# K as the moving operand, row softmax and two score banks in a decode kernel that streams a key/value cache

## The chip, the cores and the metric

The kernel runs on one core of one Trainium2 chip. The metric is the device time of one execution in microseconds. A core has five engines that matter here: TensorE (PE, with its weight loads as PEld), VectorE (DVE), ScalarE (ACT), GpSimd (POOL) and SyncE (SP), which issues every DMA of this kernel. SBUF and PSUM are the two on-chip memories, each of 128 partitions[...].

## The reference

Two transformer layers with the same weights and the same cache, for one new token of each of 8 batches:

```python
def _A_ref(x, k_cache, v_cache, wq, wo):
    q = (x @ wq).reshape(B, 1, 32, 128).transpose(0, 2, 1, 3)
    scores = jnp.einsum("bhqd,bhkd->bhqk", q, k_cache) * (128 ** -0.5)
    p = softmax(scores, axis=-1)
    o = jnp.einsum("bhqk,bhkd->bhqd", p, v_cache)
    return o.transpose(0, 2, 1, 3).reshape(B, 1, 32 * 128) @ wo
def _B_ref(x, w1, w2):
    return jnp.maximum(x @ w1, 0) @ w2
x = x + _A_ref(_layernorm(x), K, V, wq, wo)
x = x + _B_ref(_layernorm(x), w1, w2)
x = x + _A_ref(_layernorm(x), K, V, wq, wo)
x = x + _B_ref(_layernorm(x), w1, w2)
```

B is 8, the model width D is 640, there are 32 heads of width 128 with 4096 keys each, and the feed-forward width is 1728. Everything is bf16. K and V together are 537 MB, and each of the two layers needs all of them.

## The kernel before

The work is cut into visits. A visit (layer, batch, pair of heads) takes the K tile and the V tile of two heads; there are 2 x 8 x 16 = 256 visits. Each tile is cut into four granules of 512 KB, 2048 bf16 values in each of the 128 partitions. The arena in SBUF has room for G = 26 granules, and the whole cache goes through it, a load (L546) taking one to eight granules that lie side by side.

A planner, `plan` (L34), writes out the order of all operations by hand, and every engine gets its part in that order. It walks over the visits: K of visit i, then V of visit i-1. After each granule that is not kept it releases the place and, where it can, issues the next load (`release`, `feed`). Between granules, `step` puts in pieces of the small work from a list of chains. After K of a visit its chain is T, M2, B, E, L, I; after V it is OG, O and, by layer, W and Y, and at the end of a layer the feed-forward part (`finish`, L186). `until` forces the pieces that must be out before the next step.

The planner keeps 21 granules of a batch from layer 0 in the arena for layer 1 (`keep`), and 3 more (STASH) outside it: each is copied out into six half-granule tiles, five PSUM banks and one SBUF tile called annex (`do_stash`, L534), and copied back just before its use (`do_unstash`, L543). So layer 1 of a batch reads 24 granules less. The visits of a batch's layer 1 begin with the head pairs that were kept; between the end of layer 0 and there stand the first two visits of the next batch (AHEAD = 2), beside which the feed-forward part of layer 0 runs.

The scores: `do_mm` (L572) takes 128 keys of K at a time as the weight (128x128) and the head's q as a moving operand of one column, 16 matmuls for a granule (L590), into one column each of the score tile `s_ps`, 128 keys down the partitions and 64 columns, 32 for each head. `s_ps` holds two visits by turns in one tile. For V (L578), P is the weight, four columns at a time, and V moves with 512 columns: four matmuls for a granule on four column tiles of the array (`tile_position`), into `o_ps`.

The softmax: M1 (L596, DVE) takes the maximum over the columns; T (L599, PE) turns it into two rows; M2 (L603, L605, DVE) takes their maximum and puts it on a 2x2 diagonal; B (L608, PE) spreads it to all partitions; E scales it (L614, ACT) and takes the exponential, once per head (L618), which gives `P_sb` in the layout that V's matmuls need. L (L623, PE) sums the columns over the partitions, I (L629, L633, DVE) adds up and inverts. OC (L637, ACT) copies `o_ps` out, OG (L642, PE) gathers its diagonal pieces, O (L652, DVE) multiplies by the inverse sum, W (L659, PE) projects with `wo`, Y (L676, DVE) adds to x. In layer 1, Q (L564) makes the two heads' q and QC (L570, ACT) copies it to `qo`.

Of the kernel before, what the change touches and what calls it, by code (L numbers as in the profile page):

```python
# [20 lines left out]
STASH = 3  # L21
# [12 lines left out]
def plan(B, NP, n_up, n_down):  # L34
# [26 lines left out]
    stash = first[G - SPARE : G - SPARE + STASH]  # L61

# [25 lines left out]
    ops, chains = [], []  # L88
# [6 lines left out]
    def stashed(which, i, g):  # L95

        x = which, visits[i][2], g
        return stash.index(x) if x in stash else None

# [9 lines left out]
    def feed():  # L109

        while at[0] < len(stream):
# [4 lines left out]
            while n < most and place(stream[at[0] + n]) == (b, p + n, keeping):  # L116
                n += 1
# [12 lines left out]
            ops.append(("load", b, p, n, u))  # L130
# [5 lines left out]
    def release(which, i, g):  # L136
# [7 lines left out]
        if visits[i][0] == 0 and stashed(which, i, g) is not None:  # L144
            ops.append(("stash", stashed(which, i, g), u))
        owner[u], freed[u] = False, at[1]
# [34 lines left out]

    def query(b, n):

        return [(10, ("Q", b, order1[n])), (0, ("QC", b, order1[n]))]
# [18 lines left out]
    for which, i in slots:  # L203
        layer, b, hp = visits[i]
        if which == "K":
            if layer == 0 and b == 0 and hp % GP == 0:
                ops.append(("Q0", hp // GP))
            if layer:
                until(("QC", b, hp))
                if order1.index(hp) + 2 < NP:  # L210
                    chains.append(query(b, order1.index(hp) + 2))
        else:
            until(("E", i))
            clock[0] = max(clock[0], ready.pop(i))
# [7 lines left out]
        if which == "K":  # L222
# [5 lines left out]
            chains.append([(1, ("T", i)), (0, ("M2", i)), (1, ("B", i)), (0, ("E", i)), (1, None), (1, ("L", i)), (0, ("I", i))])  # L228
# [27 lines left out]
def kernel(  # L256
# [26 lines left out]
    GJ = GW // P  # L283
# [64 lines left out]
    ones_b = _free(onesb_c[:2], [(0, P)])  # L348
# [11 lines left out]
    qo = consts.tile([P, B, H], BF16, name="qo")  # L360
    wo_sum = sm.tile([P, 2, 2, 2], BF16, name="wo_sum", bufs=1)
    OR = 96 + CJ
    o_ps = ps.tile([P, CJ * Dh], FP32, name="o_ps")
    s_ps = ps.tile([P, 2, 2 * NJ], FP32, name="s_ps")
    small_ps = ps.tile([P, BANK], FP32, name="small_ps")
    oy_ps, sum_ps, mean_ps, var_ps = (small_ps[:, lo:hi] for lo, hi in ((0, 48), (48, 56), (64, 72), (72, 80)))
    turn_ps, max_ps, q1_ps = small_ps[:2, 80 : 80 + P], small_ps[:, 208:210], small_ps[:, 212:216]
    lsum_ps, ffn_ps, row_ps = small_ps[:, 216 : 216 + 2 * NJ], small_ps[:, 280:440], small_ps[:, 280 : 280 + P]
    per = GW // (2 * BANK)
    stash = [ps.tile([P, 2 * BANK], BF16, name=f"stash{n}_ps") for n in range(STASH * per - 1)]  # L370
# [5 lines left out]
    s_tiles, P_tiles, m_tiles, o_tiles, oy, invL, oT, nmax, st = ({} for _ in range(9))  # L376
# [168 lines left out]
    def do_load(b, p, n, u):  # L545
        nc.sync.dma_start(out=arena[:, u * GW : (u + n) * GW], in_=A_kv[b, :, p * GW : (p + n) * GW])  # L546
# [22 lines left out]
    def take_q(b, hp):  # L569
        nc.scalar.copy(out=qo[:, b, 2 * hp : 2 * hp + 2], in_=st.pop(("q", b, hp)))  # L570

    def do_mm(which, i, g, u):  # L572
# [11 lines left out]
        if g == 0:  # L584
            s_tiles[i] = s_ps[:, i % 2]
        h = 2 * hp + g * 2 // UNIT
        q = qo[:, b, h : h + 1]
        for n in range(GJ):
            j = g * GJ + n
            nc.tensor.matmul(  # L590
                s_tiles[i][:, j : j + 1], lhsT=arena[:, at + n * P : at + (n + 1) * P], rhs=q, start=True, stop=True
            )

    def do_m1(i):
        m_tiles[i] = sm.tile([P, 2], BF16, name="mrow")
        nc.vector.tensor_reduce(out=m_tiles[i], in_=s_tiles[i].rearrange("p (h j) -> p h j", h=2), axis=AX.X, op=ALU.max)  # L596

    def do_t(i):
        nc.tensor.matmul(turn_ps, lhsT=m_tiles.pop(i), rhs=ident, start=True, stop=True)  # L599

    def do_m2(i):
        hmx = sm.tile([2, 1], FP32, name="hmx")
        nc.vector.tensor_reduce(out=hmx, in_=turn_ps, axis=AX.X, op=ALU.max)  # L603
        nmax[i] = sm.tile([2, 2], BF16, name="diag")
        nc.vector.tensor_tensor(out=nmax[i], in0=ident[:2, :2], in1=_free(hmx, [(0, 2)]), op=ALU.mult)  # L605

    def do_b(i):
        nc.tensor.matmul(max_ps, lhsT=ones_b, rhs=nmax.pop(i), start=True, stop=True)  # L608

    def do_e(i):  # L610
        nm = sm.tile([P, 2], FP32, name="nmax")
        layer, b, hp = visits[i]
        less, more = (q_scale[b][:, 1:2], q_scale[b][:, 0:1]) if layer else (-inv_sqrt_dh, inv_sqrt_dh)
        nc.scalar.activation(out=nm, in_=max_ps, func=ACT.Copy, scale=less)  # L614
        P_tiles[i] = sm.tile([P, 2, NJ], BF16, name="P_sb")
        S = s_tiles.pop(i).rearrange("p (h j) -> p h j", h=2)
        for h in range(2):
            nc.scalar.activation(  # L618
                out=P_tiles[i][:, h, :], in_=S[:, h, :], func=ACT.Exp, bias=nm[:, h : h + 1], scale=more
            )  # L620

    def do_l(i):
        nc.tensor.matmul(  # L623
            lsum_ps, lhsT=ones_p, rhs=P_tiles[i].rearrange("p h j -> p (h j)"), start=True, stop=True
        )

    def do_i(i):
        L = sm.tile([P, 2], FP32, name="lsum")
        nc.vector.tensor_reduce(  # L629
            out=L, in_=lsum_ps.rearrange("p (h j) -> p h j", h=2), axis=AX.X, op=ALU.add  # L630
        )
# [3 lines left out]
    def do_oc(i):  # L635
        o_tiles[i] = sm.tile([P, CJ, Dh], BF16, name="o_sb", bufs=1)
# [35 lines left out]
    def do_y(i):  # L672
# [6 lines left out]
                L=do_l, I=do_i, OC=do_oc, OG=do_og, O=do_o, W=do_w, Y=do_y, C=do_finish, Q0=do_q0, Q=do_q, QC=take_q)  # L679
# [17 lines left out]
def _laid_out(A_x, A_k_cache, A_v_cache, A_wq, A_wo, B_w1, B_w2):  # L697
# [9 lines left out]
    k = A_k_cache.reshape(B, NP, 2, Sk, Dh).transpose(0, 1, 4, 2, 3).reshape(B, NP, Dh, 2 * Sk)  # L707
# [39 lines left out]
```

## Time and profile before

| what | value |
| --- | --- |
| median of three runs | 2364.6 us (2361.87 to 2365.31) |
| profiled execution | 2369.0 us, of which 2367.1 us are the profile's span |
| TensorE matmuls busy | 1300.1 us, 55%; 26,522 instructions |
| TensorE weight loads busy | 796.9 us, 34%; 26,522 instructions |
| DVE, ACT, POOL busy | 393.9, 394.6 and 39.3 us |
| read from HBM | 988.08 MB, 417 GB/s over the span |
| loads into the arena | 536: 236 of 512 KB, 127 of 4096 KB, the rest between |

Times are microseconds from the start of the span. A group of the profile gives the line, the engine, the operation, what it writes and reads, how often, its busy time, the mean of one in nanoseconds, and the idle time of the engine ahead of it with the cause of its end. TensorE's matmuls overlap, and their ends are modelled: sixteen matmuls of 165 ns can lie within 0.56 us. A turn is the stretch, once per batch, in which layer 0 of the batch ends and its layer 1 begins; they lie near 205, 490, 785, 1070, 1365, 1645, 1945 and 2215 us.

### The profile page before, as it was taken

Reading aid. Unit: us, or ns where it says so; the run is one execution under the profiler, and the core shown is the slowest. Engines: PE = TensorE matmul, PEld = TensorE weight load, DVE = VectorE, ACT = ScalarE, POOL = GpSimd, SP = SyncE. Lnnn points to the kernel's source line nnn. Section 1 sums busy time; section 2 is a strip of 40 time slices with the busy share of each in tenths; the row PEclk is TensorE's granted clock in tenths of the full one; section 3 lists DMA queues with packets and bytes.
Section 4 is the critical chain, followed back from the end, with each engine's and each line's share of the span. In section 5 each row is a group of like instructions: output and inputs, shape, how many; then the busy total and the mean of one; then the engine's idle time right before and its main releaser. Section 6 shows DMA issues by size and latency. Waiting matters only on the chain.

```text
span 2367.1 us, 57911 instructions
## 1 busy us (share of the span) xinstructions
PE 1300.1 (55%) x26522; PEld 796.9 (34%) x26522; DVE 393.9 (17%) x1913; ACT 394.6 (17%) x1185; POOL 39.3 (2%) x190
## 2 busy tenths in 40 slices
PE   3437644575545854448444585446744466544855
PEld 2324322343323532225222353223422244222533
DVE  1112111121112211122111221112211122112211
ACT  1111211121111211112111121111211112111211
POOL 0000000000000000000000000000000000000000
DMA  9999999999999999999999999999999999999997
GB/s 409 428 430 385 433 428 433 429 387 433 429 432 428 392 433 429 433 425 391 432 431 431 416 406 432 430 430 408 423 432 431 430 404 427 432 431 428 383 432 303
DMA packets 78969, 991.83 MB, mean 419 GB/s; under 512 B 8836, under 2 KB 8836, under 8 KB 39044
## 3 DMA queue, kind: packets, MB, share of 16 engines
q1 hardware_dynamic: 78724, 988.13, 98.8%
q8 instruction: 207, 3.39, 0.5%
q14 instruction: 38, 0.31, 0.0%
HBM read 988.08 MB, written 0.01 MB: 417 GB/s over the span
## 4 chain that ended last, share of the span: by engine, by line
DMA 75%; PE 18%; ACT 3%; DVE 2%; issue 1%; SPq 0%; DVEq 0%; ACTq 0%
DMA arena<-in_A_kv_dram 75%; PE s_ps L590 8%; PE o_ps L578 4%; ACT P_sb L618 2%; PE small_ps L564 1%; PE small_ps L642 1%; ACT nmax L614 1%; PE small_ps L468 1%; DVE hmx L603 1%; PE small_ps L659 1%; PE small_ps L623 1%; PE small_ps L608 1%; PE small_ps L599 0%; PE small_ps L494 0%; DVE diag L605 0%
## 5 line engine op out<-in xcount | busy, mean ns | idle before, releaser
L578 PE MATMUL o_ps<-arena,P_sb 128*4 128x512 bf16 x4096 | 564.2, 600 | 595.9 <-DMA arena<-in_A_kv_dram 595.0
L590 PE MATMUL s_ps<-qo,arena 128*128 128x1 bf16 x16384 | 535.4, 165 | 381.6 <-DMA arena<-in_A_kv_dram 360.2
L590 PEld LDWEIGHTS <-arena 128*128 128x128 bf16 x16384 | 495.8, 104 | 406.2 <-DMA arena<-in_A_kv_dram 380.4
L578 PEld LDWEIGHTS <-P_sb 128*4 128x4 bf16 x4096 | 89.6, 81 | 665.1 <-issue 650.0
L614 ACT ACTIVATE nmax<-small_ps 128x2 f32<-128x2 f32 x128 | 22.0, 172 | 1047.2 <-PE small_ps L608 1047.2
L629 DVE TENSOR_REDUCE lsum<-small_ps 128x2 f32<-128x64 f32 x256 | 57.3, 224 | 715.4 <-PE small_ps L623 715.4
L637 ACT CAST o_sb<-o_ps 100x512 bf16<-100x512 f32 x256 | 149.8, 585 | 105.5 <-PE o_ps L578 102.6
L614 ACT ACTIVATE nmax<-small_ps,q_scale 128x2 f32<-128x2 f32 x128 | 33.5, 262 | 640.6 <-PE small_ps L608 640.6
L603 DVE TENSOR_REDUCE hmx<-small_ps 2x1 f32<-2x128 f32 x256 | 71.4, 279 | 312.2 <-PE small_ps L599 312.2
L596 DVE TENSOR_REDUCE mrow<-s_ps 128x2 bf16<-128x64 f32 x256 | 57.6, 225 | 380.1 <-PE s_ps L590 351.7
L623 PEld LDWEIGHTS <-onesb_c 128*128 128x128 bf16 x256 | 26.4, 103 | 199.3 <-issue 199.2
L618 ACT ACTIVATE P_sb<-s_ps,nmax,q_scale 128x32 bf16<-128x32 f32 x256 | 82.6, 373 | 4.2
L652 DVE TENSOR_TENSOR oT<-small_ps,invL 128x2 bf16<-128x2 f32 x128 | 20.3, 159 | 312.2 <-PE small_ps L642 312.2
L642 PE MATMUL small_ps<-gsel,o_sb 100*128 100x2 bf16 x1024 | 66.3, 169 | 8.3 <-DVE xc L511 1.8
L599 PE MATMUL small_ps<-ident,mrow 128*2 128x128 bf16 x256 | 70.5, 276 | 0.2 <-DVE mrow L596 0.2
L564 PE MATMUL small_ps<-xq,wq_sb 128*128 128x1 bf16 x1280 | 52.1, 165 | 32.1 <-DVE qo L652 26.8
L564 PEld LDWEIGHTS <-wq_sb 128*128 128x128 bf16 x1280 | 52.9, 104 | 45.3 <-issue 44.4
L608 PEld LDWEIGHTS <-onesb_c 2*128 2x128 bf16 x256 | 25.2, 98 | 116.0 <-issue 115.7
L623 PE MATMUL small_ps<-P_sb,onesb_c 128*128 128x64 bf16 x256 | 57.2, 223 | 8.8
L618 ACT ACTIVATE P_sb<-s_ps,nmax 128x32 bf16<-128x32 f32 x256 | 59.4, 283 | 4.1
L642 PEld LDWEIGHTS <-o_sb 100*128 100x128 bf16 x1024 | 49.7, 108 | 25.5 <-ACT o_sb L637 10.0
L659 PE MATMUL small_ps<-oT,wo_sb 128*128 128x1 bf16 x1280 | 52.0, 165 | 4.1 <-DVE oT L652 2.4
(184 smaller groups left out, 559.3 us busy)
## 6 DMA issues: line engine op xcount, KB each, us to landing
arena<-in_A_kv_dram SPq DMA_DIRECT2D x127, 4096.0 KB, 24.5
arena<-in_A_kv_dram SPq DMA_DIRECT2D x93, 2048.0 KB, 23.3
arena<-in_A_kv_dram SPq DMA_DIRECT2D x236, 512.0 KB, 6.6
arena<-in_A_kv_dram SPq DMA_DIRECT2D x40, 1024.0 KB, 10.9
arena<-in_A_kv_dram SPq DMA_DIRECT2D x16, 2560.0 KB, 23.0
arena<-in_A_kv_dram SPq DMA_DIRECT2D x24, 1536.0 KB, 24.7
wq_sb<-in_A_wq_dram SPq DMA_DIRECT2D x4, 1280.0 KB, 29.9
wo_sb<-in_A_wo_dram SPq DMA_DIRECT2D x4, 1280.0 KB, 29.8
```

Of the source, the lines that this page charges most:

```text
L564: nc.tensor.matmul(q_ps[:, h : h + 1], lhsT=wq_sb[:, g, c, (2 * n + h) * Dh : (2 * n + h + 1) * Dh], rhs=xlns[b][:, 0, c : c + 1], start=( ...
L578: nc.tensor.matmul(o_ps[32 * c : 32 * c + CJ, :], lhsT=P_tiles[i][:, h, j : j + CJ], rhs=arena[:, at + c * CJ * Dh : at + (c + 1) * CJ * D ...
L590: nc.tensor.matmul(s_tiles[i][:, j : j + 1], lhsT=arena[:, at + n * P : at + (n + 1) * P], rhs=q, start=True, stop=True)
L596: nc.vector.tensor_reduce(out=m_tiles[i], in_=s_tiles[i].rearrange("p (h j) -> p h j", h=2), axis=AX.X, op=ALU.max)
L599: nc.tensor.matmul(turn_ps, lhsT=m_tiles.pop(i), rhs=ident, start=True, stop=True)
L603: nc.vector.tensor_reduce(out=hmx, in_=turn_ps, axis=AX.X, op=ALU.max)
L614: nc.scalar.activation(out=nm, in_=max_ps, func=ACT.Copy, scale=less)
L618: nc.scalar.activation(out=P_tiles[i][:, h, :], in_=S[:, h, :], func=ACT.Exp, bias=nm[:, h : h + 1], scale=more)
L623: nc.tensor.matmul(lsum_ps, lhsT=ones_p, rhs=P_tiles[i].rearrange("p h j -> p (h j)"), start=True, stop=True)
L637: nc.scalar.copy(out=o_tiles[i][:OR], in_=o_ps[:OR, :].rearrange("p (j d) -> p j d", j=CJ))
L642: nc.tensor.matmul(oy[i][:, :2], lhsT=o_tiles[i][:OR, j, :], rhs=gsel[:OR, j, :], start=(j == 0), stop=(j == CJ - 1))
L659: nc.tensor.matmul(oy[i][:, 2 + c * nb : 2 + (c + 1) * nb], lhsT=wo_sb[:, 2 * hp + h, c * P : (c + 1) * P], rhs=qo[:, :, 2 * hp + h] if la ...
```

## The change

K moves. For each granule `do_mm` now makes four matmuls on the four column tiles, with 512 keys of K as the moving operand and q as the weight. The weight is a window of four columns in `qz`, in which one column is q and the others are zero: for granule g, q stands in column g, so that the four granules of a tile add up in four rows of one PSUM bank without touching each other's. The scores of a visit are then rows: four groups (head, half of 1024 keys) of four rows (granule) with 512 columns. The two visits that are under way have a PSUM bank each (`s_ps[0]`, `s_ps[1]`). K is laid out on the host so that a granule holds 1024 keys of both heads.

The softmax goes by rows: M1 reduces 512 columns, T turns 16 numbers into one row with a selection matrix `rsel`, M2 takes two maxima, B spreads them with two matmuls of 64 rows each, and E is one exponential over 100 partitions and 512 columns into `P_row`. V still needs P with the keys down the partitions: PT turns `P_row` with four matmuls against `rsel`, and PC (DVE) copies the result into `P_sb`. V of a visit now waits for PC instead of E, and the place for two pieces in the chain (B, and an empty one) becomes B with two matmuls and PT with four. `P_row` and `o_sb` share one buffer.

q has to be in `qz`, which has room for three visits: in layer 1 QC writes there, in layer 0 a new operation QZ (POOL) copies it from `qo`, up to two visits ahead.

The score tiles take one more PSUM bank, so five half granules are kept outside the arena instead of six: STASH is 2, and of one more granule (`half`) the first half goes to annex; its other half is loaded by a DMA of 256 KB.

```diff
-STASH = 3
+STASH = 2
...
+    half = first[G - SPARE + STASH]
...
+    def halved(which, i, g):
+
+        return visits[i][0] == 1 and (which, visits[i][2], g) == half
...
+            part = halved(*stream[at[0]])
+            while n < most and not part and place(stream[at[0] + n]) == (b, p + n, keeping) and not halved(*stream[at[0] + n]):
...
+            if part:
+                ops.append(("unstash", STASH, u))
+            ops.append(("load", b, p, n, u, part))
...
+        if visits[i][0] == 0 and (which, visits[i][2], g) == half:
+            ops.append(("stash", STASH, u))
...
+    def pad(i):
+
+        for i in range(i, min(i + 3, NV)):
+            layer, b, hp = visits[i]
+            if layer == 0 and i not in done and ("Q0", hp // GP) in done:
+                ops.append(("QZ", i))
+                done.add(i)
...
-            until(("E", i))
+            until(("PC", i))
...
-            chains.append([(1, ("T", i)), (0, ("M2", i)), (1, ("B", i)), (0, ("E", i)), (1, None), (1, ("L", i)), (0, ("I", i))])
+            chains.append([(1, ("T", i)), (0, ("M2", i)), (2, ("B", i)), (0, ("E", i)), (4, ("PT", i)), (0, ("PC", i)),
+                           (1, ("L", i)), (0, ("I", i))])
...
+    rsel = sm.tile([P, 4 * CJ], BF16, name="rsel", bufs=1)
+    nc.vector.memset(rsel, 0.0)
...
+    qz = sm.tile([P, 3, 2, 8], BF16, name="qz", bufs=1)
+    nc.vector.memset(qz, 0.0)
...
-    s_ps = ps.tile([P, 2, 2 * NJ], FP32, name="s_ps")
+    s_ps = [ps.tile([P, BANK], FP32, name=f"s{n}_ps") for n in range(2)]
+    for t in s_ps:
+        nc.vector.memset(t, -1e30)
...
-        nc.scalar.copy(out=qo[:, b, 2 * hp : 2 * hp + 2], in_=st.pop(("q", b, hp)))
+        nc.scalar.copy(out=qz[:, visits.index((1, b, hp)) % 3, :, 3], in_=st.pop(("q", b, hp)))
...
-        for n in range(GJ):
-            j = g * GJ + n
+        for c in range(4):
             nc.tensor.matmul(
-                s_tiles[i][:, j : j + 1], lhsT=arena[:, at + n * P : at + (n + 1) * P], rhs=q, start=True, stop=True
+                s_ps[i % 2][32 * c : 32 * c + CJ, :], lhsT=qz[:, i % 3, c // 2, 3 - g : 3 - g + CJ],
+                rhs=arena[:, at + c * BANK : at + (c + 1) * BANK],
+                start=(g == 0), stop=(g == UNIT - 1), tile_position=(0, 32 * c),
             )
 
+    def do_qz(i):
+        layer, b, hp = visits[i]
+        nc.gpsimd.tensor_copy(out=qz[:, i % 3, :, 3], in_=qo[:, b, 2 * hp : 2 * hp + 2])
+
     def do_m1(i):
-        m_tiles[i] = sm.tile([P, 2], BF16, name="mrow")
-        nc.vector.tensor_reduce(out=m_tiles[i], in_=s_tiles[i].rearrange("p (h j) -> p h j", h=2), axis=AX.X, op=ALU.max)
+        m_tiles[i] = sm.tile([P, 1], BF16, name="mrow")
+        nc.vector.tensor_reduce(out=m_tiles[i][:OR], in_=s_ps[i % 2][:OR], axis=AX.X, op=ALU.max)
 
     def do_t(i):
-        nc.tensor.matmul(turn_ps, lhsT=m_tiles.pop(i), rhs=ident, start=True, stop=True)
+        nc.tensor.matmul(turn_ps, lhsT=m_tiles.pop(i)[:OR], rhs=rsel[:OR], start=True, stop=True)
...
-        nc.tensor.matmul(max_ps, lhsT=ones_b, rhs=nmax.pop(i), start=True, stop=True)
+        mx = nmax.pop(i)
+        for h in range(2):
+            nc.tensor.matmul(
+                max_ps[64 * h : 64 * (h + 1)], lhsT=ones_h, rhs=mx[:, h : h + 1], start=True, stop=True,
+                tile_position=(0, 64 * h),
+            )
...
-        for h in range(2):
-            nc.scalar.activation(
-                out=P_tiles[i][:, h, :], in_=S[:, h, :], func=ACT.Exp, bias=nm[:, h : h + 1], scale=more
-            )
+        P_rows[i] = sm.tile([P, BANK], BF16, name="P_row", tag="row", bufs=1)
+        nc.scalar.activation(out=P_rows[i][:OR], in_=s_ps[i % 2][:OR], func=ACT.Exp, bias=nm[:OR], scale=more)
+
+    def do_pt(i):
+        P_row = P_rows.pop(i)
+        for k in range(BANK // P):
+            nc.tensor.matmul(
+                P_ps[:, k * 4 * CJ : (k + 1) * 4 * CJ], lhsT=P_row[:OR, k * P : (k + 1) * P], rhs=rsel[:OR],
+                start=True, stop=True,
+            )
+
+    def do_pc(i):
         P_tiles[i] = sm.tile([P, 2, NJ], BF16, name="P_sb")
+        nc.vector.tensor_copy(
+            out=P_tiles[i].rearrange("p h (c k) -> p h c k", k=BANK // P),
+            in_=P_ps.rearrange("p (k h c) -> p h c k", k=BANK // P, h=2),
+        )
```

## The prediction

> **What bounds the kernel now.** I read the page from the top: the DMA queues, the chain of waits, the costliest groups. Then I asked for busy time by stage, for the DMA view of one stage, and for TensorE's timeline in two places.
>
> ```profile
> q1 hardware_dynamic: 78724, 988.13, 98.8%
> q8 instruction: 207, 3.39, 0.5%
> ...
> DMA 75%; PE 18%; ACT 3%; DVE 2%; issue 1%; SPq 0%; DVEq 0%; ACTq 0%
> ...
> L578 PE MATMUL o_ps<-arena,P_sb 128*4 128x512 bf16 x4096 | 564.2, 600 | 595.9 <-DMA arena<-in_A_kv_dram 595.0
> L590 PE MATMUL s_ps<-qo,arena 128*128 128x1 bf16 x16384 | 535.4, 165 | 381.6 <-DMA arena<-in_A_kv_dram 360.2
> ...
> L637 ACT CAST o_sb<-o_ps 100x512 bf16<-100x512 f32 x256 | 149.8, 585 | 105.5 <-PE o_ps L578 102.6
> ```
>
> The cache's queue is busy for 98.8% of the span and carries 75% of the chain, so the stream of K and V is the bound. The second queue, q8, fetches instructions: 3.39 MB is 64 bytes for each of TensorE's 53,044 instructions (26,522 matmuls, as many weight loads), in packets of 16 KB.
>
> ```profile
> 240.00:480.00 240.00, 120.03 (x2426) 69.39 (x2423) 36.18 (x172) 38.21 (x116) 0.00 (x0) 1.00 1.00 431
> 480.00:520.00 40.00, 31.74 (x667) 22.69 (x667) 7.98 (x47) 5.70 (x20) 4.83 (x23) 1.00 0.97 369
> ```
>
> The columns are stage, length, busy time of PE, PEld, DVE, ACT and POOL, clock, DMA share, GB/s. The quiet stretch of a batch runs at 431 GB/s with TensorE half idle. In the turn from layer 0 to layer 1, once a batch, TensorE is 79% busy and the stream falls to 369.
>
> ```profile
> GB/s 418 397 414 422 414 422 414 414 393 254 217 213 324 348 340 270 254 254 385 373 418 418 381 393 385 344 336 328 340 418 414 422 401 418 401 360 401 385 434 410
> ...
> 303.07 0.60 PE L578 MATMUL o_ps<-arena,P_sb 128*4 128x512 bf16 x4 [7.56 <-DMA arena<-in_A_kv_dram]
> 314.31 0.60 PE L578 MATMUL o_ps<-arena,P_sb 128*4 128x512 bf16 x4 [6.04 <-DMA arena<-in_A_kv_dram]
> 324.00 1.44 PE L590 MATMUL s_ps<-qo,arena 128*128 128x1 bf16 x48 [1.19 <-DMA arena<-in_A_kv_dram]
> 333.66 0.60 PE L578 MATMUL o_ps<-arena,P_sb 128*4 128x512 bf16 x4 [7.57 <-DMA arena<-in_A_kv_dram]
> ```
>
> The first line is that turn in 1 us slices: from 489 us the rate is about 213, half the usual, as if half of the engines had run out while the others finished. The rest is TensorE starting on landed data, each interval 4 MB: 11.24, 9.69, 9.66 us. The long one contains an instruction fetch (at 310.0), but so does 314 to 324 (at 322.4). The next long interval, 414.78 to 426.01, contains the fetch at 419.3, the eighth after it. So I read: fetches go round eight of the sixteen engines, each sets one back by some 1.5 us, and a load counts as landed only with its slowest engine. Eight fetches cost the stream about 1.3 us.
>
> [...] first and last of the sixteen landings lie 3.7 us apart near 303 us, 5.3 us at 314. [...] four V matmuls of 512 columns end 0.60 us after the first begins[...].
>
> **The change part by part.** *Fetches.* A K granule goes from 16 matmuls with 16 weight loads to 4 and 4, over 1024 granules: 24,576 instructions fewer. Each of 256 visits gains one matmul with its load for the second half of B, and four for turning P: 2,560 more. 31,028 remain: 1.99 MB, 121 packets instead of 207. The price of a fetch: over the seven quiet stretches between turns, the last landings come 22.8 us later in all than at the undisturbed rate (4 MB in 9.69 us), with 138 fetches in them: 0.165 us each. 86 x 0.165 = 14.2 us saved. The other reading spreads q8's share over all engines: 0.5% of 2367 is 11.8 us, 0.057 each, 4.9 us saved. I take 14.2, because the steps of 1.2 to 1.55 us come with every eighth fetch, which an even spread would not give.
>
> *Half a granule less is kept.* One PSUM bank goes to the scores, so each batch reads 256 KB more: 8 x 256 KB at 433 GB/s (4 MB in 9.69 us) is 4.8 us, 5.0 with the shorter packets. It is on the path in full; nothing hides a byte on a full queue. The loads are cut differently too (549 instead of 536); packets of 4 KB still land at 1.22 us per granule against 1.21, so 13 more loads are nothing. The half load is layer 1's first in SP's queue and moves nothing else there. Of the stash, DVE copies one piece less out and one less back per batch.
>
> *The chain of a visit.* M1 reduces 100x512 instead of 128x64 (224 ns): between 0.49 (DVE's memset of a PSUM tile 512 wide) and 0.61 (the slope between the 64- and 128-wide reductions, 224 and 279 ns, carried on to 512); I take 0.6. T and M2 turn 16 numbers instead of 128 and lose the diagonal product: 0.3 us less. One exponential of 100x512, by the row of the o_sb copy 0.585, replaces two of 283 or 373 ns. PT is four matmuls like the four of the o gather, 0.27 us together; PC a DVE copy like the 128x64 row, 0.22. In sum the way from scores to P grows by 0.6 us, with two more handovers 0.9. In the quiet stretch a visit lasts 9.7 us and TensorE waits 5 to 7 us on landings: hidden; without that cover it would be 256 x 0.9. POOL's 128 copies of q (about 0.2 us) are asked for up to two visits ahead: hidden. Only POOL's root chain shares its queue.
>
> *TensorE in the turn.* Here sixteen single loads go round in five free buffers, and each load is issued when a granule is done, so TensorE's pace counts. A granule with its feed-forward slice takes about 1.21 us, as DMA does.
>
> ```profile
> 496.98 0.54 PE L468 MATMUL small_ps<-xf,w_sb 128*128 128x1 bf16 x15
> 497.45 0.18 PE L608 MATMUL small_ps<-diag,onesb_c 2*128 2x2 bf16 x1
> 498.39 0.57 PE L590 MATMUL s_ps<-qo,arena 128*128 128x1 bf16 x16 [0.76 <-ACT P_sb L618]
> ...
> 500.54 0.23 PE L623 MATMUL small_ps<-P_sb,onesb_c 128*128 128x64 bf16 x1
> 501.54 0.60 PE L578 MATMUL o_ps<-arena,P_sb 128*4 128x512 bf16 x4 [0.76 <-DMA arena<-in_A_kv_dram]
> ```
>
> A K granule holds TensorE 0.45 us before the next slice, a V granule 0.53; K becomes like V: 6 x 0.08 = +0.48. T -0.2, the second B +0.2, PT +0.54 for two visits. The wait of 0.76 on ACT goes: I read it as the scores of two visits sharing one tile. In its place PT waits for the exponential; B to its end is some 1.15 us, a K granule covers 0.6 to 0.7: +0.45, and the feed-forward slice behind PT waits with it. Sum +0.71 per turn. TensorE already waits on DMA 0.76 at 501.54, which covers part: I take half, 3 us over eight turns; bounds 0 (all covered) and 6 (none). Unstashing the half granule holds ACT about 1.0 us (its copy of this shape has 1018 ns) ahead of one o copy per batch; TensorE is ahead of the stream by then: nothing. The start gains some 2 us of memsets, ahead of a first weight load that TensorE awaits for 1.9: nothing. The end, 13.7 us after the last landing, holds only V and feed-forward work.
>
> Sum: -14.2 + 5.0 + 3.0 = -6.2. The profiled execution took 2369.0 (span 2367.1 and 1.9 around it): 2362.8 there. The median lies 4.4 below it, so the forecast is 2358 us.
>
> **The rivals.** *TensorE's turn decides (slower).* Place: the sixteen loads of each turn. If wide K granules slow their neighbours by 0.12 rather than 0.08 each over eight of them (1.0), PT and T wait in both visits (1.0 and 0.4), PT costs its 0.5 and little is covered, a turn loses some 2.6 us after the old wait is credited: -14.2 + 5.0 + 21 = +11.8, 2376. It outweighs the saving from 1.15 us per turn. For it: TensorE 79% busy there and issue tied to its pace; against it: the DMA waits that remain. Chance 0.28. *Fetches cost only their average.* -4.9 + 5.0 + 3.0 = +3: 2368, no measurable change. For it: q8's share is just 0.5%; against it: the half-rate slices. Chance 0.14. *Fetches cost more in the turn.* With few loads outstanding a late engine holds up the next issue: some 1 us each instead of 0.165. About 1.3 fewer per turn then give another 8 to 9 us, and TensorE's term is covered: 2347. Chance 0.08. That the instructions are not saved is excluded by the count.
>
> **How the numbers follow.** The likeliest, 0.50, is 2358 with its own range 2350 to 2364 from the bounds of its terms. Two of ten may lie outside 2343 to 2378, which takes in both ends. A change of 0.2%, 4.7 us, is about what a measurement of this kernel can tell from none. Faster: 0.45 of the first case and 0.08, 0.53; within: 0.05, 0.11 of the average case and 0.03 of the slower one, 0.19; slower: 0.25 and 0.03, 0.28.
>
> **What would show it.** q8 at about 121 packets and 2.0 MB; q1 at 990.2 MB; quiet stretches with the lengthened 4 MB interval about every 190 us instead of 110; a shorter half-rate dip at the turn's start; no wait of K on ACT in the turn, one of PT instead, near 0.45 us. I am wrong if quiet stretches keep their pace though the packets fell, or if the turn's gaps between landings exceed 1.22 us at every granule: then TensorE sets the pace.

## The result and the profile after

The changed kernel takes 2380.2 us (median of four executions, 2374.4 to 2383.0) against 2365.0 (2361.9 to 2367.7) for the kernel before, measured beside it: a ratio of 1.0062, 95% interval 1.0037 to 1.0086. In a second session it took 2377.4, ratio 1.0062 [1.0050, 1.0074]. It is slower by about 0.6%, some 13 to 15 us, where the forecast was 2358 and a range up to 2378. The case that came in is the first rival, TensorE's turn, at 2376.

The profiled execution took 2374.4 us, 2372.7 of them its span. From its page, the TensorE clock in 40 slices, the queues, the chain that ended last (shares by engine), and the groups that answer to those of before:

```profile
PEclk9999999999555555555555555555555555555555
...
q1 hardware_dynamic: 80596, 990.22, 99.1%
q8 instruction: 121, 1.98, 0.3%
...
DMA 64%; PE 23%; ACT 6%; DVE 4%; issue 2%; SPq 0%; ACTq 0%; DVEq 0%; POOL 0%; POOLq 0%
...
L617 PE MATMUL s_ps<-arena,qz 128*4 128x512 bf16 x4096 | 546.4, 597 | 447.5 <-DMA arena<-in_A_kv_dram 444.5
L610 PE MATMUL o_ps<-arena,P_sb 128*4 128x512 bf16 x4096 | 608.5, 593 | 211.6 <-DMA arena<-in_A_kv_dram 205.6
L629 DVE TENSOR_REDUCE mrow<-s_ps 100x1 bf16<-100x512 f32 x256 | 177.7, 694 | 320.2 <-PE s_ps L617 320.2
...
L657 PE MATMUL small_ps<-rsel,P_row 100*128 100x16 bf16 x1024 | 70.3, 179 | 139.6 <-ACT P_row L652 139.5
...
L652 ACT ACTIVATE P_row<-s_ps,nmax,q_scale 100x512 bf16<-100x512 f32 x128 | 99.5, 778 | 4.2
```

The counts came as forecast: 121 instruction packets of 1.98 MB, 990.22 MB through the cache's queue. The queue is even a little fuller than before, 99.1%, but DMA's share of the chain has fallen from 75% to 64%, with ScalarE's and VectorE's up to 6% and 4%: the stretches in which the stream doesn't decide have grown. The page's clock line stands at half from about 590 us on; the page of before has no such line. What that means is taken up behind the experiments.

Those stretches lie in and behind each turn. In the chain of before, in the execution shown ahead of the prediction, the part from 508 to 530 us contains 7.68 us of waiting for a landing; in the same stretch of after no piece is a landing. In a second execution of before (b0) there is none either: TensorE's pace set these visits before the change too, and the change made them longer. From the chain of waits of after (start us, length us, what):

```profile
518.09 0.69 DVE mrow L629
518.78 0.14 DVE lsum L674
518.92 0.04 issue
518.96 0.17 PE small_ps L632
519.13 0.44 PE o_ps L610 x4
519.57 0.16 PE small_ps L641 x2
519.76 0.27 ACT nmax L650
520.03 0.03 issue
520.05 0.79 ACT P_row L652
520.84 0.05 issue
520.88 0.27 PE small_ps L657 x4
```

This is one softmax chain, M1, T, B, E, PT, with a V granule (L610) between T and B, and the kernel goes at its pace. TensorE's own timeline shows what it waits for (start us, us, engine, line, what; in brackets the idle time ahead of it and its cause):

```profile
496.76 0.27 PE L657 MATMUL small_ps<-rsel,P_row 100*128 100x16 bf16 x4 [0.44 <-ACT P_row L652]
497.42 0.63 PE L499 MATMUL small_ps<-xf,w_sb 128*128 128x1 bf16 x10 [0.38 <-DVE P_sb L664]
...
510.89 0.24 PE L685 MATMUL small_ps<-gsel,o_sb 100*128 100x2 bf16 x4 [0.80 <-ACT qz L602]
...
514.51 0.17 PE L632 MATMUL small_ps<-rsel,mrow 100*1 100x16 bf16 x1 [0.38 <-DVE mrow L629]
...
517.24 0.28 PE L657 MATMUL small_ps<-rsel,P_row 100*128 100x16 bf16 x4 [0.70 <-ACT P_row L652]
...
520.88 0.27 PE L657 MATMUL small_ps<-rsel,P_row 100*128 100x16 bf16 x4 [0.65 <-ACT P_row L652]
```

The first two are the waits of PT for the exponential and of the feed-forward slice for PC, in the first of the two visits of layer 0 that open the turn. The third is the gather behind a copy on ScalarE that brings back the half granule. The last three belong to layer 1's visits behind the turn, whose granules were kept, all but half of one: next to nothing has to land for them, and a visit lasts as long as TensorE and its chain need. From one L (column sums of P) to the next, visits there take 5.21, 5.50 and 5.21 us in the second execution of the kernel before, and 6.85 and 6.75 in after. Three such starts of each (L623 is L of before, L670 of after):

```profile
517.32 0.21 PE L623 MATMUL small_ps<-P_sb,onesb_c 128*128 128x64 bf16 x1
522.53 0.21 PE L623 MATMUL small_ps<-P_sb,onesb_c 128*128 128x64 bf16 x1
528.03 0.21 PE L623 MATMUL small_ps<-P_sb,onesb_c 128*128 128x64 bf16 x1
...
521.62 0.23 PE L670 MATMUL small_ps<-P_sb,onesb_c 128*128 128x64 bf16 x1
528.47 0.23 PE L670 MATMUL small_ps<-P_sb,onesb_c 128*128 128x64 bf16 x1
535.22 0.23 PE L670 MATMUL small_ps<-P_sb,onesb_c 128*128 128x64 bf16 x1
```

SyncE waits for them, as its waits between 505 and 530 us in after show (engine, line, waited for: us in total, times, longest):

```profile
SPq L578 <- PE s_ps L617: 4.0, 3, 2.9
SPq L578 <- PE small_ps L670: 3.8, 2, 1.9
SPq L578 <- PE small_ps L641: 2.6, 2, 1.4
...
```

Every load that waits there waits for TensorE to let go of a place. In the quiet stretch SyncE waits for TensorE too (from 240 to 480 us 34 times, 137.7 us in all), but there a load of 4 MB lands 23.1 us after its issue (median), a single one 5.9 us after it: here a late issue has little time to be made up.

To say where time is lost I took, from the landing records, how much later each load's last landing came than its size takes at the undisturbed rate (4 MB in 9.69 us), and summed it over the eight windows around the turns (each from 50 us ahead of the first single load to 40 us behind the last) and over the rest. The border is not sharp; differences of 2 us mean little. Of before there are two rows of numbers because the profiled execution shown ahead of the prediction took 4 us longer than its median and a second one (b0) took 2361.4.

| kernel, profiled execution | in turns | elsewhere | last landing |
| --- | --- | --- | --- |
| before, two executions | 39.6, 34.1 | 21.6, 19.7 | 2353.4, 2345.8 |
| after, two executions | 48.8, 49.9 | 12.9, 14.4 | 2357.5, 2360.4 |
| before with the half granule, ScalarE copies (e1) | 42.1 | 20.8 | 2360.0 |
| before with the half granule, DVE copies (e7) | 37.2 | 20.3 | 2354.7 |
| after, DVE copies (e2) | 40.7 | 16.8 | 2353.3 |
| after with idle matmuls (e4) | 54.6 | 23.8 | 2374.5 |
| after, M1 and E twice in four visits per batch (e9) | 78.9 | 17.4 | 2392.2 |
| K as weight in six visits per batch (e12) | 37.4 | 12.2 | 2345.8 |

Outside the turns the change gains 7 us in the mean, near what the forecast's price gives for the fetches saved there; in the turns it loses more.

### The profile page after: what moved, and what is told of

It is laid out like the page before. It is cut to its first block, busy times and chain, and to the rows that moved or that the text cites. A ratio compares the mean times of both kernels' runs of the same rounds, so it can differ in the third digit from the quotient of the medians.

```text
span 2372.7 us, 36413 instructions
## 1 busy us (share of the span) xinstructions
PE 1431.2 (60%) x15514; PEld 517.6 (22%) x15514; DVE 497.3 (21%) x1905; ACT 441.3 (19%) x929; POOL 63.8 (3%) x318
## 3 DMA queue, kind: packets, MB, share of 16 engines
q1 hardware_dynamic: 80596, 990.22, 99.1%
q8 instruction: 121, 1.98, 0.3%
## 4 chain that ended last, share of the span: by engine, by line
DMA 64%; PE 23%; ACT 6%; DVE 4%; issue 2%; SPq 0%; ACTq 0%; DVEq 0%; POOL 0%; POOLq 0%
DMA arena<-in_A_kv_dram 64%; PE s_ps L617 8%; PE o_ps L610 6%; ACT P_row L652 3%; DVE mrow L629 3%; PE small_ps L596 2%; ACT o_sb L680 1%; PE small_ps L657 1%; PE small_ps L685 1%; ACT nmax L650 1%; PE small_ps L525 1%; PE small_ps L499 1%; PE small_ps L702 1%; PE small_ps L641 1%; PE small_ps L632 1%
## 5 line engine op out<-in xcount | busy, mean ns | idle before, releaser
L617 PE MATMUL s_ps<-arena,qz 128*4 128x512 bf16 x4096 | 546.4, 597 | 447.5 <-DMA arena<-in_A_kv_dram 444.5
L610 PE MATMUL o_ps<-arena,P_sb 128*4 128x512 bf16 x4096 | 608.5, 593 | 211.6 <-DMA arena<-in_A_kv_dram 205.6
L629 DVE TENSOR_REDUCE mrow<-s_ps 100x1 bf16<-100x512 f32 x256 | 177.7, 694 | 320.2 <-PE s_ps L617 320.2
L617 PEld LDWEIGHTS <-qz 128*4 128x4 bf16 x4096 | 89.7, 86 | 509.8 <-issue 486.5
L610 PEld LDWEIGHTS <-P_sb 128*4 128x4 bf16 x4096 | 111.3, 89 | 326.0 <-issue 311.9
L664 DVE CAST P_sb<-small_ps 128x64 bf16<-128x64 f32 x256 | 57.4, 224 | 542.5 <-PE small_ps L657 542.5
L657 PE MATMUL small_ps<-rsel,P_row 100*128 100x16 bf16 x1024 | 70.3, 179 | 139.6 <-ACT P_row L652 139.5
L657 PEld LDWEIGHTS <-P_row 100*128 100x128 bf16 x1024 | 47.0, 107 | 264.3 <-ACT P_row L652 264.2
L652 ACT ACTIVATE P_row<-s_ps,nmax,q_scale 100x512 bf16<-100x512 f32 x128 | 99.5, 778 | 4.2
L695 DVE TENSOR_TENSOR oT<-small_ps,invL 128x2 bf16<-128x2 f32 x128 | 20.3, 159 | 348.3 <-PE small_ps L685 348.3
L652 ACT ACTIVATE P_row<-s_ps,nmax 100x512 bf16<-100x512 f32 x128 | 87.9, 687 | 4.1
L632 PE MATMUL small_ps<-rsel,mrow 100*1 100x16 bf16 x256 | 46.1, 180 | 69.9 <-DVE mrow L629 67.9
## 6 DMA issues: line engine op xcount, KB each, us to landing
arena<-in_A_kv_dram SPq DMA_DIRECT2D x117, 4096.0 KB, 23.1
```

The costliest lines, as they stand in the source:

```text
L610: nc.tensor.matmul(o_ps[32 * c : 32 * c + CJ, :], lhsT=P_tiles[i][:, h, j : j + CJ], rhs=arena[:, at + c * CJ * Dh : at + (c + 1) * CJ * D ...
L617: nc.tensor.matmul(s_ps[i % 2][32 * c : 32 * c + CJ, :], lhsT=qz[:, i % 3, c // 2, 3 - g : 3 - g + CJ], rhs=arena[:, at + c * BANK : at + ...
L629: nc.vector.tensor_reduce(out=m_tiles[i][:OR], in_=s_ps[i % 2][:OR], axis=AX.X, op=ALU.max)
L632: nc.tensor.matmul(turn_ps, lhsT=m_tiles.pop(i)[:OR], rhs=rsel[:OR], start=True, stop=True)
L652: nc.scalar.activation(out=P_rows[i][:OR], in_=s_ps[i % 2][:OR], func=ACT.Exp, bias=nm[:OR], scale=more)
L657: nc.tensor.matmul(P_ps[:, k * 4 * CJ : (k + 1) * 4 * CJ], lhsT=P_row[:OR, k * P : (k + 1) * P], rhs=rsel[:OR], start=True, stop=True,)
```

## The experiments

The ratios are to the kernel before, on the same chip in the same session; it took 2362.8 to 2364.1 us there.

**The kernels again, and the half granule alone (b0, e1, e7, e10).** e1 is the kernel before with the half granule of the change and nothing else of it; e7 lets DVE instead of ScalarE bring it back; e10 keeps two whole granules outside the arena and loads the other half too, so it has twice the bytes and no odd copy. A PSUM bank is here a tile of up to 512 fp32 (`BANK`) or 1024 bf16 values per partition. The kernel before lays out eight such tiles, one of them for the scores and five for half granules, and after lays out eight too, two for the scores and four for half granules; no run lays out a ninth, so that the second score tile must cost half a granule was my premise, which nothing here shows.

```diff
# e1 and e7, from before; e10 has only STASH = 2 and no annex
-STASH = 3
+STASH = 2
+    half = first[G - SPARE + STASH]
...
# e7
-            copy = nc.vector.tensor_copy if n % 2 else nc.scalar.copy
+            copy = nc.vector.tensor_copy if n % 2 or slot == STASH else nc.scalar.copy
```

After again:

> The changed kernel itself, again, beside the others on one chip. Theory A (new waits of TensorE in the turns cost about 15 us and eat the 14 us that fewer instruction fetches save; the half granule costs its 5 us): ratio to before 1.004 to 1.008, each turn's loads land 5 to 7 us late, quiet stretches 13 us late in all. Theory B (the half granule that is no longer kept costs two or three times its bytes) and theory C (the granted TensorE clock, which falls to 0.5, slows the turns) expect the same ratio; C also expects a slower run where the clock falls earlier.

Before again:

> The kernel before, again, on the same chip as the others of this call, so that its turns and quiet stretches can be compared with theirs in one profile of a usual length. All theories: ratio 1.000; quiet stretches 21 to 22 us late in all, turns 33 to 38 us.

e1:

> The kernel before with only two and a half granules kept outside the arena and the half load of 256 KB, nothing else of the change. Theory A: the bytes alone, 8 x 256 KB at 433 GB/s, +5 us, ratio 1.002 (1.001 to 1.003). Theory B: +10 to +15 us, ratio 1.004 to 1.006. Theory C: +5 us, with the clock left at 1.0.

e7:

> The kernel before with the half granule, copied back by DVE instead of ACT. If what the half granule costs above its bytes (11.6 us measured, 5 of them bytes) is ACT's copy of 1.04 us ahead of the o copy in each turn: +5 to +6 us over before, ratio 1.002. If it is the other plan of loads, or a load of 256 KB as such: still +10 to +12 us, ratio 1.0045 or more.

e10:

> The kernel before with two granules kept outside the arena instead of three and no half load: 8 x 512 KB more, 9.7 us by bytes at 433 GB/s, nothing copied in between and the first load of layer 1 a whole granule. If the half granule costs more than its bytes because of the short load or its copies: +9 to +11 us over before, 2373 to 2375. If every granule that is not kept costs half as much again as its bytes: +14 to +16, 2378 to 2380.

Measured: after again 1.0062 [1.0050, 1.0074]; before again 0.9999 [0.9991, 1.0007]; e1 2375.7, 1.0050 [1.0038, 1.0062], 11.6 us over before; e7 2371.4, 1.0034 [1.0022, 1.0046], 7.6 over; e10 2374.7, 1.0046 [1.0034, 1.0059], 11.9 over. So the half granule alone costs nearly as much as the whole change loses. By bytes it should be 4.8 (2.09 MB more through q1, at 433 GB/s), and e10, with twice of them, 9.7: e10 lies 2.2 above, e7 2.8 above, between its two expectations. The rest of e1, 4.0 us (over chips), is the copy on ScalarE. e1's timeline of TensorE shows its trace (columns as above):

```profile
512.02 0.24 PE L653 MATMUL small_ps<-gsel,o_sb 100*128 100x2 bf16 x4 [0.90 <-ACT qo L581]
```

And ScalarE in the same place:

```profile
510.38 1.04 ACT L553 COPY arena<-annex 128x1024 bf16<-128x1024 bf16 x1 [2.06 <-PE o_ps L589]
511.33 0.58 ACT L648 CAST o_sb<-o_ps 100x512 bf16<-100x512 f32 x1
511.81 0.16 ACT L581 CAST qo<-small_ps 128x2 bf16<-128x2 f32 x1
```

The copy waits for a V matmul to free its place, then keeps ScalarE for 1.04 us; o_sb's copy and layer 1's q queue behind it, and TensorE's gather waits 0.90 us for both. All of it is in a profile without any record of a halved clock, with K still as the weight.

**The copy, in the changed kernel (e2).** The same line as in e7, in after.

> The changed kernel with the half granule copied back by DVE instead of ACT, so that the copy of o after a batch's turn no longer stands behind a 1.04 us copy on ACT. Theory A: the wait of 0.80 us of the gather OG in each turn goes or shrinks to 0.3, 3 to 7 us less than the changed kernel. Theories B and C: no change, within 2 us.

2372.3 us, 1.0033 [1.0021, 1.0045]: 5.1 less than after on that chip. The gather's wait of 0.80 is gone from the timeline. Eight copies of about 1 us each return 5: TensorE's pace counts there, and the stream doesn't cover it.

**The price of an instruction fetch (e4).** After, with 12 matmuls that nobody reads added to each K granule of the quiet visits.

```diff
+        if 3 <= hp <= (12 if layer else 11):
+            for n in range(12):
+                nc.tensor.matmul(small_ps[:, 504:505], lhsT=ident, rhs=onesb_c, start=True, stop=True)
```

> The changed kernel with twelve idle one-column matmuls and their weight loads added to each K granule of the visits far from the turns (about 19 of 32 per batch): some 14,600 instructions more, 57 fetches of 16 KB. TensorE has 5 us or more to spare in each of these visits. If a fetch costs the stream 0.165 us: +9 us over the changed kernel, all in the quiet stretches. If it costs its average over sixteen engines, 0.057: +3 us. If fetches are free: 0. [...]

2393.4 us, 1.0126 [1.0113, 1.0139]: 16 more than after, where 9 had been expected at the forecast's price. The page's line for the instruction fetches (packets, MB, share):

```profile
q8 instruction: 178, 2.92, 0.4%
```

57 fetches more, 53 of them outside the turns, where the lateness grows from 14.4 (after again) to 23.8: 9.4, or 0.18 us per fetch; from the 12.9 of the first execution of after it would be 0.21. The turns grew by 4.7 and the end by 1.5, which these fetches don't explain; a share of the 16 us is probably the idle work itself, which this run can't tell from the fetches. The other way round, the profiles with K as the weight throughout (six) have 124 fetches outside the turns and 21.0 us of lateness there in the mean, after and its relatives without added work (seven) 71 and 13.5: 7.5 us for 53, 0.14 each. The forecast's 0.165 lies between. These are differences of a few us with borders that aren't sharp; they lie above an even spread, 0.057 each, which would have given 3, but they don't fix the second digit.

**PT later (e3, e6).** The chain's order has PT one granule further back, so that the exponential is ready when TensorE comes to it; the last line keeps PC ahead of OC, as P_row and o_sb share one buffer. e6 is e3 with DVE's copy of the half granule.

```diff
-            chains.append([(1, ("T", i)), (0, ("M2", i)), (2, ("B", i)), (0, ("E", i)), (4, ("PT", i)), (0, ("PC", i)),
-                           (1, ("L", i)), (0, ("I", i))])
+            chains.append([(1, ("T", i)), (0, ("M2", i)), (2, ("B", i)), (0, ("E", i)), (1, None), (4, ("PT", i)), (0, ("PC", i)),
+                           (1, None), (1, ("L", i)), (0, ("I", i))])
...
+            until(("PC", i + 1))
```

> The changed kernel with PT one place later (after the fourth V granule, ahead of OC) and L one place later than PT, so that PT no longer stands behind the exponential. Theory A, waits of TensorE in the turns: PT's 139.5 us of waiting on P_row falls by more than half, the turns' loads come earlier by 0.5 to 1 us each, 4 to 8 us less than the changed kernel. If the turn is not bound by these waits but by the loads' way through five buffers: no change, within 2 us.

> The changed kernel with both: the half granule copied back by DVE, and PT and L later. Theory A: the two add up, 9 to 13 us less than the changed kernel, ratio to before 0.9995 to 1.002. If PT's wait is not in the way: as with DVE's copy alone, ratio 1.003.

2378.1, 1.0061 [1.0048, 1.0074], and 2371.3, 1.0036 [1.0024, 1.0049]: no gain over after and over e2. TensorE's waits in after (waited for: us in total, times, longest):

```profile
PE small_ps L657 <- ACT P_row L652: 139.5, 247, 1.7
PE small_ps L632 <- DVE mrow L629: 67.9, 182, 0.4
```

And in e3:

```profile
PE small_ps L686 <- DVE lsum L675: 77.0, 233, 2.7
PE small_ps L633 <- DVE mrow L630: 68.0, 184, 0.5
PE small_ps L658 <- ACT P_row L653: 30.9, 125, 1.3
```

PT's wait falls by 109 us, and 77 come back at the gather (L686), which now waits behind L; T's wait for M1 is as it was. A visit of layer 1 behind the turn has only eight granules on TensorE to lie beside the chain, so a piece put later meets the next one; that is the likely reason, read from the waits alone.

**The chain's length (e8a, e8b, e9).** All three from e2. e8a and e8b shorten M1 and E in some visits: M1 reads 64 columns, E makes 128 and PT turns those four times. e8a does it in the first four of a batch's visits of layer 1, e8b in the two visits of layer 0 ahead of them. e9 makes M1 and E twice in e8a's visits.

```diff
# e8a; e8b has the condition b and not layer and hp < 2
+        n = 64 if layer and hp in (15, 14, 13, 0) else BANK
+        nc.vector.tensor_reduce(out=m_tiles[i][:OR], in_=s_ps[i % 2][:OR, :n], axis=AX.X, op=ALU.max)
...
+        n = P if layer and hp in (15, 14, 13, 0) else BANK
+        nc.scalar.activation(out=P_rows[i][:OR, :n], in_=s_ps[i % 2][:OR, :n], func=ACT.Exp, bias=nm[:OR], scale=more)
...
# e9, around M1 and around E
+        for n in range(2 if layer and hp in (15, 14, 13, 0) else 1):
```

> The changed kernel with DVE's copy of the half granule, and in the first four visits of layer 1 of each batch (the second part of the turn) M1 takes 64 of the 512 columns, the exponential 128, and PT turns those 128 four times: a part of the softmax is left out, with the same number of instructions. It takes about 0.45 us off M1 and 0.4 off the exponential, 0.8 to 0.9 us of TensorE's waits in each visit. If these waits hold back the loads: 4 to 9 us less than the 2372 with DVE's copy. If the time of the turn is set ahead of these visits, or by the loads' way alone: within 2 us of it.

> The same, but in the two visits of the next batch that stand in the first part of the turn, beside the feed-forward work. TensorE waits there 0.44 us for P_row and 0.38 for PC in one visit. If these waits hold back the loads: 2 to 5 us less than 2372. If TensorE has the time there, as it waits on landings near by: within 2 us.

> The changed kernel with DVE's copy, and M1 and the exponential done twice in the first four visits of layer 1 of each batch: about 1.4 us more of waits per visit, 5.5 per turn. If these waits hold back the loads one to one: +25 to +40 us over 2372; if half of it: +10 to +20. If TensorE has room there: within 3 us.

e8a 2364.3, 1.0005 [0.9996, 1.0013]; e8b 2366.9, 1.0018 [1.0009, 1.0026]; e9 2409.6, 1.0199 [1.0185, 1.0213]. Each taken against the kernel before on its chip, and then against e2, that is -6.7, -4.2 and +38.6 us (over chips, so to a us or two). In e9 the two repeats take 0.694 and 0.778 us by the page of after, in 32 visits 47 us: a us added to the chain there costs 0.8 us of time. The way back returns less. In e8a M1 takes 0.226 and E 0.458 us, 25 us less of chain in 32 visits, and 6.7 come back, 0.3 of each; in e8b it is 11 us less in 14 visits, and 0.4 of each. Which limit takes over when the chain gets shorter isn't shown. Shortened, the layer's visits take 5.8 us from L to L instead of 6.4 to 6.5, and TensorE's timeline of e8a has half the wait:

```profile
523.39 0.27 PE L661 MATMUL small_ps<-rsel,P_row 100*128 100x16 bf16 x4 [0.33 <-ACT P_row L655]
```

None of this could be had if the stream still covered the chain there. Elsewhere it covers most of it: after's 247 waits of PT sum to 139.5 us, and the kernel lost 13.

**Both forms of K (e12, e13).** From e2. In six visits per batch, e8a's four and e8b's two, K is the weight as before, with the column softmax and without PT; in the others K moves. e13 does so in ten visits.

```diff
+    def down(i):
+
+        layer, b, hp = visits[i]
+        return hp in (15, 14, 13, 0) if layer else b > 0 and hp < 2
...
+        if down(i):
+            for n in range(GW // P):
+                h, j = n // VJ, g * VJ + n % VJ
+                nc.tensor.matmul(
+                    s_ps[i % 2][:, h * NJ + j : h * NJ + j + 1], lhsT=arena[:, at + n * P : at + (n + 1) * P],
+                    rhs=qz[:, i % 3, h, 3:4], start=True, stop=True,
+                )
+            return
# e13
-        return hp in (15, 14, 13, 0) if layer else b > 0 and hp < 2
+        return hp in (15, 14, 13, 0, 1, 2) if layer else hp > 13 or b > 0 and hp < 2
```

> The changed kernel with DVE's copy, and in six visits of each turn (two of layer 0, four of layer 1) K is the weight again, with the column softmax of the kernel before; elsewhere K moves. If the loss lies in the new chain and the wide granules of these visits: the turns fall to those of the kernel before or below (no wait for the other visit's scores either), the quiet stretches keep their 7 us from fewer fetches, 10 to 16 us less than the 2372 with DVE's copy, ratio to before 0.9975 to 0.9995. If the loss lies elsewhere: ratio 1.002 or more.

> As the run before, with two more visits ahead of the turn and two behind it, ten per batch. If TensorE's pace matters there too: 2 to 5 us less than with six visits. If not: within 2 us, or 1 to 3 us more, for the fetches of four more visits with K as the weight.

e12 takes 2358.2 us (18 executions), 0.9985 [0.9977, 0.9993]: less than both kernels; each against before on its chip, it is 11 to 13 us better than e2, with only six visits per batch put back. e13 takes 2361.1, 0.9993 [0.9984, 1.0001]; the intervals overlap, and four more visits bring nothing that can be seen. They cost 11 fetches (q8 has 147 packets, in e12 136), 1.8 us at 0.165, which is as much as e13 lies above e12 (1.9 by the ratios). TensorE's timeline of e12 at the place where after waits:

```profile
518.20 0.21 PE L715 MATMUL small_ps<-P_sb,onesb_c 128*128 128x64 bf16 x1
518.23 0.59 PE L627 MATMUL s_ps<-qz,arena 128*128 128x1 bf16 x16
518.82 0.27 PE L730 MATMUL small_ps<-gsel,o_sb 100*128 100x2 bf16 x4
519.33 0.41 PE L604 MATMUL small_ps<-xq,wq_sb 128*128 128x1 bf16 x10 [0.25 <-DVE qo L740]
519.60 1.42 PE L627 MATMUL s_ps<-qz,arena 128*128 128x1 bf16 x48
```

A visit there is back to 5.2 to 5.5 us. A sum for it is 71 fetches fewer than before at 0.165, -11.7, and +7.6 for the half granule: -4.1; the ratio gives -3.5, the medians -4.6. That they agree doesn't prove each term: the two score tiles, which come next, are not in the sum.

**The two score tiles alone (e14).** From e7: the scores of two visits in two tiles of 64 columns.

```diff
-    s_ps = ps.tile([P, 2, 2 * NJ], FP32, name="s_ps")
+    s_ps = [ps.tile([P, 2 * NJ], FP32, name=f"s{n}_ps") for n in range(2)]
```

> The kernel before with the half granule copied by DVE (2371 us) and the scores of the two visits in two tiles, a PSUM bank each: K of the next visit no longer waits for the exponential and M1 of the visit ahead, 0.76, 1.09 and 0.3 us in each turn. At half to nine tenths of these waits, as the doubled chain suggests: 8 to 15 us less, 2356 to 2363. If those waits were covered: within 2 us of 2371.

2368.6, 1.0025 [1.0014, 1.0035]: about 2 us less than e7, each against before on its chip, with intervals that overlap; 8 to 15 had been expected. In e7 K's matmuls wait 16 times for P_sb, 16.0 us in all; in e14 that wait is gone. So its end is worth about an eighth of it, if anything. That most of it lay beside landings is the likely reason; no run shows it by itself.

## Why the prediction was wrong

The forecast's three terms were -14.2, +5.0 and +3.0. The runs give, in medians: the half granule 11.6 in before (e1), of which 7.6 remain with DVE's copy; then all else of the change, e1 to after, +1.7, or e7 to e2, +0.6 (over chips). With the fetches at -14.2, the rest, which the forecast had as TensorE's term, is 15 to 16; it is as sure as the price of a fetch.

- **Fetches, -14.2: right as far as it can be seen.** 121 packets came as counted, and the price lies between 0.14 and 0.21 us. 53 of the 86 were saved outside the turns, where 7 us show in the landings (8.7 at 0.165). What the other 33 saved in the turns no run shows by itself. That a fetch goes to one of eight engines in turn and sets it back by some 1.5 us was my estimate from the intervals between landings; the runs show only what fetches cost.
- **Half a granule, +5.0: too small, and in two parts.** The bytes came as counted, 990.22 MB, and e10 with twice of them costs 11.9. The part put at nothing was the copy back. The forecast said "Unstashing the half granule holds ACT about 1.0 us ... TensorE is ahead of the stream by then: nothing". The duration was right (1.04), the "nothing" was the error: TensorE is ahead of the landings there, so it is what frees the places that SyncE waits for. It cost 4 to 5 us, shown by e1 against e7 and by e2. Some 2.8 us of e7 above the bytes are not explained.
- **TensorE in the turn, +3.0: the step that failed.** It was sized for two visits, "PT waits for the exponential ... +0.45", and half of it was taken as covered. There the reading was good: in the first of the two visits PT waits 0.44 us, with 0.38 behind it for PC, in the second (502.62) not at all, and K's wait on ScalarE is gone. But the same chain runs in the visits of layer 1 that follow, and these were not counted at all: the working took the turn to end with "sixteen single loads", the granules of the two visits. In the trace of before 29 loads of 512 KB stand in a row there, issued from 465 to 517 us. In layer 1's visits the waits are larger (0.65 to 0.70 for E, 0.37 to 0.38 for M1), in part because with q_scale the exponential takes 778 ns where I had taken the 585 of a copy, and M1 694 where I had taken 600. That the loss lies in these six visits per batch is shown by e12, which puts them back to the old form and gains 11 to 13 us over e2. That the chain's length is part of it is shown by e8a (6.7 us, layer 1) and e8b (4.2, layer 0). These two leave out parts of the softmax rather than go back to the old chain, so their sum doesn't divide up the 15 to 16.
- **"In the quiet stretch ... hidden": right** for the time, though PT waits 247 times in the trace.
- **The end.** It was said to hold only V and feed-forward work. From the last landing to the end of the span after takes 15.2 us and the kernel before 13.7: 1.5 us that were not in the sum. The last V granule starts at the landing in before and 1.5 us behind it in after, where PT has waited 0.65 us for the exponential at 2355.49: the same chain once more.
- **The rival** had the engine and came near in its total, 2376, but in part by luck. It had +21 in the turns, 2.6 us in each, from waits of PT and T in both visits; the terms that it names (1.0, 1.0, 0.4 and 0.5, less the 0.76 credited) sum to 2.1, which gives 17. Lateness in the turns rose by 9 to 16 us although 33 fetches fewer fall there (5.4 us at 0.165), which makes 15 to 21. Some of that is the half granule's copy, which the rival had not in it. It too counted two visits only.
- **What was to show it.** "I am wrong if ... the turn's gaps between landings exceed 1.22 us at every granule": they don't, most single loads still land 1.2 to 1.3 us after the one before; the loss comes in a few late ones per turn (at 504.32 us after 501.87, at 517.59 after 515.33). The mark was too strict: the stream is late where a single place comes free late, not at every granule.

The halved clock is not the cause. The trace of after has its first record of the granted clock at 580.26 us, and that of before has none; where no record is, the page counts 1.0. The matmuls tell the pace. Twelve of K in a row in after, first where no record is, then in the 3.4 us from 580.26 that are recorded at 1.0, then where 0.5 is recorded:

```profile
523.56 1.45 PE L617 MATMUL s_ps<-arena,qz 128*4 128x512 bf16 x12
...
583.04 0.87 PE L617 MATMUL s_ps<-arena,qz 128*4 128x512 bf16 x12
...
1091.27 1.45 PE L617 MATMUL s_ps<-arena,qz 128*4 128x512 bf16 x12
```

Over all profiles in which K moves, groups of four K matmuls that follow at once begin 378 to 428 ns apart at a recorded 0.5 (all 2981), 378 to 440 where no record is (415 of 416), and about 215 ns apart in the short stretches recorded at 1.0 (104 of 112). In the six profiles with K as the weight throughout, which have no record at all, groups of V begin 378 to 385 ns apart (all 1390). So what the pages give as 1.0 and 0.5 was one pace but for those stretches of 3.4 or 6.8 us, and the change did not slow TensorE's clock. e1 loses its 11.6 us without any record of 0.5, and e12, which has them, is faster than before.

Open are: what e7 pays above its bytes; how the rest of e2's turns divides between waits and the wider K granules; and whether the chain still costs anything in the four further visits of e13, where the fetches alone account for the difference.

## What to carry to other kernels

Before a wait is costed at nothing because an engine is ahead of the stream, ask who frees the stream's buffers there: where the next load waits for that engine, a us added to its small chains can cost most of a us (0.8 in e9), though a us taken away returned only 0.3 to 0.4 (e8a, e8b). Such a stretch can outlast the loads that mark it: here by the first four visits of layer 1 (e8a, e12); that the next two count isn't shown (e13). A form that saves instructions everywhere and lengthens a chain can be kept for the stretches where the chain is hidden, and the old form used in the few visits where it isn't (in e12, 46 of 256 visits; with DVE's copy they make the step from +0.33% to -0.15%). A wait that is moved by reordering must be looked for again at the next matmul of the same chain (in e3 PT's fell by 109 us, and 77 came back at the gather).

## What the runs showed of the hardware

- In after an exponential of 100x512 from PSUM to bf16 takes 687 ns with its scale as a constant and 778 ns with the scale read from SBUF; the copy of the same shape takes 587.
- A page's clock of 1.0 can mean that no record was taken (in after up to 580.26 us, in before throughout). Here groups of four matmuls of 512 columns began about 383 or 427 ns apart both without a record and at a recorded 0.5, and 215 ns apart only in stretches recorded at 1.0, 3.4 or 6.8 us each.
- A fetch of 16 KB of instructions beside a stream that fills the sixteen engines costs some 0.14 to 0.21 us by these runs, about three times its share of the queues' time (0.057).
- A matmul on loaded data began just behind the last of the load's sixteen landings: in before the sixteen of one load came from 299.32 to 303.02 us, and TensorE began at 303.07; those of the next load of 4 MB came from 309.00 to 314.27, and TensorE began at 314.31.
